# The last row of w_down in two halves with 64-column matmuls, and the last 4 MB of w_o as one load

One core of one Trainium2 chip. The metric is the device time of one execution in microseconds, lower is better. In the views PE is the matrix engine (PEld its weight loads), DVE the vector engine, ACT the scalar engine, and SP the one whose queue issues the loads. A matmul is two records: LDWEIGHTS for one operand, the weights, and MATMUL for the other, the moving operand.

## The reference, cut to what matters

One decode step of a block: adaLN modulation, attention over a cache of 65,536 positions, output projection with w_o, layer norm, then a gated feed-forward layer. The change touches the last line, and the projection with `wo` before it.

```python
x = x + ga * _A_ref(h, A_k_cache, A_v_cache, A_wq, A_wo)      # wo: 4096 x 1024
h = _layernorm(x, axis=-1) * (1 + cb) + sb
x = x + gb * _B_ref(h, B_w_gate, B_w_up, B_w_down)            # w_down: 3584 x 1024
```

There is one token, so every product is a vector by a matrix, and the kernel is a stream of 185.6 MB of weights and cache out of HBM.

## The kernel before

The weights go to ten slots of 2 MB. A load is planned in order, and SP issues it once the slot's last readers are done. `w_down` is used in 28 "rows" of 128 x 1,024: rows 0 to 19 as the moving operand against a 32-column weight ("row form"), the last eight as the weights themselves ("column form"):

```python
def col_matvec(bank, jobs, rhs, nblk, first):          # column form; nblk = KD = 8, D = 1024
    for (jb, view, k0, nk) in jobs:
        PE.wait(jb.tok)
        for kk in range(nk):
            for j in range(nblk):
                ins = pe.matmul(
                    bank[:, j:j + 1], view[:, kk, j:D:nblk], rhs[:, k0 + kk:k0 + kk + 1], ...)
        tok = PE.done(ins)
        release(jb, tok)
    ...
```

`view[:, kk, j:D:nblk]` is the weight: 128 columns, each 8 elements from the next, so that output `8 p + j` lands in partition `p`, column `j`. The moving operand is one column. The end of the kernel:

```python
v = row_matvec(place_d, early, o_pad, (v_uc,), ...)     # rows 0 to 19
# ... DVE transposes the sums of the row form (1.3 us)
late = j_d[len(early):]                                 # loads of rows 20-21, 22-23, 24-25, 26, 27
col_matvec(acc_dn, late[:1], o_pad[:, :, 0], KD, True)
PE.wait(v_rows, v_sel)
for a in range(NQ):                                     # adds the transposed sums to acc_dn
    pe.matmul(acc_dn[QD * a:QD * (a + 1), :], sel32[:, :], turned[:, a, :, 0], ...)
v = col_matvec(acc_dn, late[1:], o_pad[:, :, 0], KD, False)
DVE.wait(v)
# ... two DVE products and sums of 128 x 8, then the output DMA
```

Of the kernel before, what the change touches and what calls it, by code (L numbers as in the profile page):

```python
# [9 lines left out]
P = 128  # L10
# [8 lines left out]
UE = 4  # L19
# [3 lines left out]
ROW = 512  # L23
# [57 lines left out]
def bass_adaLN_cond__gqa_block_cached__geglu_ffn__decode_kernel(  # L81
# [14 lines left out]
    D = A_x.shape[-1]  # L96
    KD = D // P
# [7 lines left out]
    FD = F // P  # L105
# [13 lines left out]
    PE = Eng(nc, nc.tensor, "c_pe")  # L119
# [3 lines left out]
    sp, pe, dve, act, pool = nc.sync, nc.tensor, nc.vector, nc.scalar, nc.gpsimd  # L123
# [24 lines left out]
    o_pad = p_row[:, :, :].rearrange("p a b -> p (a b)").rearrange("p (k c) -> p k c", c=QD)  # L148
# [41 lines left out]
    acc_dn = b7[:, 64:64 + KD]  # L190
# [9 lines left out]
    def plan_load(src, view_fn, slot, site=None, nslot=1, beside=None, off=0, sem=None):  # L200

        if site is not None:
            site.n += 16
            tok = (site.sem, site.n)
        else:
            sem = slot if sem is None else sem
            nfill[sem] += 1
            tok = (fill[sem], 16 * nfill[sem])
        job = Job(view_fn(slot_all[:, slot * SLOT + off:(slot + nslot) * SLOT]), tok, slot)
        job.src = src  # L210
        job.freed = None
        job.prev = []
        if beside is not None:
            job.prev = beside.prev
        for t in range(slot, slot + (nslot if beside is None else 0)):
            if last_job[t] is not None and last_job[t] not in job.prev:
                job.prev.append(last_job[t])
            last_job[t] = job
        loads.append(job)
        return job  # L220
# [3 lines left out]
    def issue_ready():  # L224

        while issued[0] < len(loads):
            j = loads[issued[0]]
            if any(q.freed is None for q in j.prev):
                return
            SP.wait(*(q.freed for q in j.prev))  # L230
            sp.dma_start(j.view, j.src).then_inc(j.tok[0], 16)
            issued[0] += 1
# [3 lines left out]
    def release(job, tok):  # L236
        job.freed = tok
        if not in_loop[0]:
            issue_ready()

    def flat(nk, n):
        return lambda t: t[:, 0:nk * n].rearrange("p (k n) -> p k n", k=nk)

    def emit_all():
# [5 lines left out]
        wo_v = A_wo.rearrange("(p k) n -> p k n", p=P)  # L250
        wg_v = B_w_gate.rearrange("(p k) n -> p k n", p=P)
        wu_v = B_w_up.rearrange("(p k) n -> p k n", p=P)
        wd_v = B_w_down.rearrange("(b p e) n -> p b e n", p=P, e=UE)
# [3 lines left out]
        def kv_src(h, i, n=1):  # L257
            g, cc = divmod(i, NCH)
            return h[g][:, cc * CH:(cc + n) * CH, :]
# [2 lines left out]
        j_mod = [(plan_load(wmod_v[:, k:k + 2, :], flat(2, M6), next(head), nslot=2), k, 2) for k in range(0, KD, 2)]  # L262
        j_q = [(plan_load(wq_v[:, k:k + 4, :], flat(4, HQ * DH), next(head), nslot=2), k, 4) for k in range(0, KD, 4)]
        tail = iter([2, 4, 6, 8])
        tail_d = iter([0, 1, 2, 3, 4, 5])

        def plan_o(k, slot):
            return (plan_load(wo_v[:, k:k + 8, :], flat(8, D), slot), k, 8)

        def vslot(j):  # L270
            return SITES + j % SITES
# [10 lines left out]
        j_o = []  # L282
        for i in range(0, NC + KU, KU):
# [6 lines left out]
            if i >= KU:  # L290
                j = i - KU
                j_v[j] = plan_load(kv_src(vh, j, VU), flat(VU * CH, DH), vslot(j), vfill[j % SITES // VU], VU)
        j_o += [plan_o(16, 0), plan_o(24, 1)]
        j_g = [(plan_load(wg_v[:, k:k + 4, :], flat(4, F), next(tail), nslot=2), k, 4) for k in range(0, KD, 4)]
        j_u = [(plan_load(wu_v[:, k:k + 4, :], flat(4, F), next(tail), nslot=2), k, 4) for k in range(0, KD, 4)]
        j_d = []
        NBF = FD // UE
        b = 0
        NROW = NBF - 2
        while b + 2 < NROW:  # L300
            jb = plan_load(
                wd_v[:, b:b + 2, :, :],
                lambda t: t[:, 0:2 * UE * D].rearrange("p (b e n) -> p b e n", b=2, e=UE),
                next(tail_d),
            )
            j_d.append((jb, jb.view.rearrange("p b e n -> p (b e) n"), b * UE, 2 * UE))
            b += 2
        while b < NBF:
            for e, ne in ((0, UE),) if b < NROW else ((0, 2), (2, 2)) if b == NROW else ((0, 2), (2, 1), (3, 1)):
                if b == NROW:  # L310
                    jb = plan_load(
                        wd_v[:, b, e:e + ne, :], flat(ne, D), jb.slot, beside=jb, off=(UE + e) * D, sem=9 - e)
                else:
                    jb = plan_load(wd_v[:, b, e:e + ne, :], flat(ne, D), next(tail_d))
                j_d.append((jb, jb.view, b * UE + e, ne))
            b += 1
# [28 lines left out]
        for a in [a for r in ev for a in r] + ex + m1 + oc + pc + kfill + vfill:  # L345
# [10 lines left out]
        v = DVE.done(dve.tensor_reduce(  # L356
            dm4.unsqueeze(3), identf[:, :].rearrange("p (c b h) -> p c b h", c=NQ, h=REP), AX.X, ALU.add))
# [8 lines left out]
        for j in range(KD):  # L366
            ins = pe.matmul(b6[:, 2 * j:2 * j + 2], cx_row[:, j:D:KD], ident[0:2, 0:2], start=True, stop=True)
        v = PE.done(ins)
# [5 lines left out]
        v = DVE.done(dve.tensor_scalar(sg_col[:, :], th_col[:, :], 0.5, 0.5, ALU.mult, ALU.add))  # L374
# [3 lines left out]
        def col_matvec(bank, jobs, rhs, nblk, first):  # L378

            tok = None  # L380
            for (jb, view, k0, nk) in jobs:
                PE.wait(jb.tok)
                ins = None
# [3 lines that stand above are left out]
                            bank[:, j:j + 1], view[:, kk, j:D:nblk], rhs[:, k0 + kk:k0 + kk + 1],  # L387
                            start=first, stop=True, skip_group_check=True,
                        )
                        first = False  # L390
                tok = PE.done(ins)
                release(jb, tok)
            return tok

        def whole(jobs):
            return [(jb, jb.view, k0, nk) for jb, k0, nk in jobs]
# [69 lines left out]
        def turn(dst, w, src, cols, n, ready):  # L466

            PE.wait(*ready)
            for i, a in enumerate(cols):
                ins = pe.transpose(dst[:, i * w:i * w + n], src[:, a], identf[0:src.shape[0], 0:n])  # L470
            return PE.done(ins)
# [37 lines left out]
        def place_2(b0, n):  # L509
            def place(k):  # L510
                for c in range(n):
                    yield quad(b0 + c // NQ, c % NQ), c * ROW
            return place

        v = row_matvec(place_2(0, 2 * NQ), whole(j_q), h_pad, (v_h,), (0, KD - 1), rest_of_mod)
# [4 lines left out]
        v = turn(tr_ps, P, row_q, plain, P, (v_ra, v_rb))  # L520
        DVE.wait(v)
        v = DVE.done(dve.tensor_copy(
            q_col[:, :].rearrange("p (r g t) -> p r t g", r=2, g=NQ),
            quads(tr_ps, KD).rearrange("p (r t) g -> p r t g", r=2)))
# [243 lines left out]
        for g in range(Hkv):  # L768
            ins = pe.matmul(
                b6[0:HQ, 0:P + ZW], selw[:, HQ - REP * (g + 1):HQ - REP * (g + 1) + QD], o_red[:, g, :],  # L770
                start=g == 0, stop=g == Hkv - 1)
        v = PE.done(ins)
        DVE.wait(v)
        v = DVE.done(dve.reciprocal(rz[:, :], b6[0:HQ, P + ZW - 1:P + ZW]))
        DVE.wait(v)
        v = DVE.done(dve.tensor_scalar(oT[:, :], b6[0:HQ, 0:P], rz[:, 0:1], None, ALU.mult))
        PE.wait(v, v_const)
        w = P // QW
        for q in range(QW):
            ins = pe.matmul(  # L780
                b6[:, 352:352 + w], spread[:, QW - 1 - q:QW - 1 - q + P], oT[:, q * w:(q + 1) * w],
                start=q == 0, stop=q == QW - 1)
        v = PE.done(ins)
# [16 lines left out]
        v = row_matvec(place_o, whole(j_o), o_pad, (v_opk,) + last_ev, (NQ - 1, HQ - NQ))  # L800
        t_att = sb("t_att", [P, KD])
        v_rows = both(row_a, 0, P)
        v = turn(tr_ps, P, row_a, mixed, P, v_rows)
# [3 lines left out]
        v = DVE.done(dve.tensor_tensor(t_att[:, :], t_att[:, :], mod_sb[:, 2, :], ALU.mult))  # L807
        DVE.wait(v)
        v_x1 = DVE.done(dve.tensor_tensor(x1_col[:, :], t_att[:, :], x_col, ALU.add))
        hn2, v = ln_norm(x1_col[:, :], v_x1, 34)  # L810
        v_h2 = modulate(h_pad, hn2, v, 3, 4)
        NBF = F // ROW
# [15 lines left out]
        v = row_matvec(place_2(2, NBF), whole(j_g), h_pad, (v_h2,), (0, KD - 1))  # L828
# [3 lines left out]
        for dst, src in zip(parts(g1), parts_ps()):  # L832
            v = DVE.done(dve.tensor_copy(dst, src))
        v_g1 = v
        DVE.wait(v)
        v = DVE.done(dve.tensor_tensor(g2, g1, g1, ALU.mult))
        DVE.wait(v)
        v = DVE.done(dve.tensor_scalar(g3, g2, GELU_C, 1.0, ALU.mult, ALU.add))
        DVE.wait(v)
        v = DVE.done(dve.tensor_tensor(g4, g3, g1, ALU.mult))  # L840
        AC.wait(v)
        v = AC.done(act.activation(gth, g4, ACT.Tanh, scale=SQRT_2_OVER_PI))
        DVE.wait(v)
        v = DVE.done(dve.scalar_tensor_tensor(g2, gth, 1.0, g1, ALU.add, ALU.mult))
        v_g2 = v
        v = row_matvec(place_2(0, NBF), whole(j_u), h_pad, (v_h2,), (0, KD - 1))
# [10 lines left out]
        v = row_matvec(place_d, early, o_pad, (v_uc,), (NQ - 1, NROW * UE - NQ))  # L857
# [5 lines left out]
        late = j_d[len(early):]  # L863
# [3 lines left out]
        for a in range(NQ):  # L867
            pe.matmul(
                acc_dn[QD * a:QD * (a + 1), :], sel32[:, :], turned[:, a, :, 0],
                start=False, stop=True, skip_group_check=True)  # L870
        v = col_matvec(acc_dn, late[1:], o_pad[:, :, 0], KD, False)
        DVE.wait(v)
        v = DVE.done(dve.tensor_tensor(t_dn, acc_dn, mod_sb[:, 5, :], ALU.mult))
        DVE.wait(v)
        v = DVE.done(dve.tensor_tensor(y_col, t_dn, x1_col[:, :], ALU.add))
# [3 lines left out]
        assert issued[0] == len(loads)  # L879

    emit_all()
    return nc

# [27 lines left out]
```

## Time and profile before

| | before |
|---|---|
| time, median of 3 runs | 437.55 us (437.49 to 437.65) |
| span of the profiled run | 436.2 us |
| HBM read | 185.60 MB, 426 GB/s over the span |
| DMA queue of the loads, share of the 16 engines | 99.0% |
| PE, DVE, ACT busy | 69%, 47%, 26% |
| last landing of w_down, to DVE's next step | 433.40 us, to 434.32 us |

The 99.0% say that the transfers set the length up to their last byte. What comes after the last landing is the loose part at this end, and it is about 2.8 us of 436.2. The views that show it stand in the prediction. A *landing* is the time at which the sixteenth and last of the DMA engines has counted up a load's semaphore. The *beat* is the time from the start of one matmul to the start of the next.

### The profile page before, as it was taken

The page shows a single profiled execution, that of the slowest core. Times are in us where ns is not written, and L with a number is a line of the kernel's source. Part 1 is how long each engine was busy: PE and PEld are TensorE (multiplying, and loading weights), DVE is VectorE, ACT ScalarE, POOL GpSimd, SP SyncE. Part 2 cuts the span into 40 slices and gives each one's busy share as a digit, 9 for nine tenths or more (in the row PEclk, how much of TensorE's full clock was granted, in tenths as well). Part 3 has the DMA queues.
Part 4 walks back from the last instruction along what each step waited for, and adds up shares of the span by engine and source line. Part 5 has one row for each costly group of instructions (what it writes and reads, how often), then busy time and mean ns, then how long its engine had stood idle before and what let it go on. Part 6 is the DMA issues. An engine that isn't in the chain of part 4 may idle for free.

```text
span 436.2 us, 8423 instructions
## 1 busy us (share of the span) xinstructions
PE 302.8 (69%) x3858; PEld 200.5 (46%) x3858; DVE 206.7 (47%) x303; ACT 111.2 (26%) x164; POOL 16.8 (4%) x23
## 2 busy tenths in 40 slices
PE   0435559959696878949787794969689596565366
PEld 0112236736464656636465563646456373232024
DVE  6601015637373755736474763738377465321001
ACT  1000001533332423333341353333235334000000
POOL 9500000000000000000000000000000000000000
PEclk9995569999796988988896897969689889578856
DMA  8999999999999999999999999999999999999996
GB/s 355 433 421 434 433 431 431 431 432 433 433 433 439 430 433 433 436 433 433 439 433 433 433 430 436 433 436 436 433 433 433 433 418 436 437 433 429 420 425 265
DMA packets 8192, 185.77 MB, mean 426 GB/s; under 512 B 1010, under 2 KB 1010, under 8 KB 1652
## 3 DMA queue, kind: packets, MB, share of 16 engines
q1 hardware_dynamic: 8176, 185.60, 99.0%
q8 instruction: 8, 0.13, 0.1%
q14 instruction: 4, 0.03, 0.0%
q10 hardware_dynamic: 4, 0.00, 0.0%
HBM read 185.60 MB, written 0.00 MB: 426 GB/s over the span
## 4 chain that ended last, share of the span: by engine, by line
DMA 56%; PE 31%; DVE 11%; issue 1%; ACT 1%; POOL 0%; POOLq 0%
DMA slots<-in_A_k_cache_dram 45%; PE kt_ps L575 16%; DMA slots<-in_B_w_down_dram 7%; PE b L645 4%; DMA slots<-in_A_v_cache_dram 4%; PE sc_ps L597 4%; PE kt_ps L409 3%; DVE selt L359 3%; DVE kt_sb L683 2%; DVE s_pad L717 1%; DVE o_red L706 1%; PE sc_ps L626 1%; PE b L613 1%; PE b L386 1%; DVE o_acc L694 1%
## 5 line engine op out<-in xcount | busy, mean ns | idle before, releaser
L575 PE MATMUL kt_ps<-ident,slots 128*128 128x128 bf16 x2048 | 156.7, 238 | 48.8 <-DMA slots<-in_A_k_cache_dram 48.0
L683 DVE COPY kt_sb<-kt_ps 128x2048 bf16<-128x2048 bf16 x96 | 117.6, 1225 | 111.5 <-PE kt_ps L575 109.9
L575 PEld LDWEIGHTS kt_ps<-ident,slots 128*128 128x128 bf16 x2048 | 136.1, 108 | 74.3 <-issue 41.9
L683 ACT ACTIVATE kt_sb<-kt_ps 128x2048 bf16<-128x2048 bf16 x32 | 60.1, 1877 | 27.7 <-PE kt_ps L575 27.7
L732 ACT ACTIVATE p_sb<-sc_ps 128x512 bf16<-128x512 bf16 x32 | 19.1, 597 | 182.4 <-PE sc_ps L626 182.4
L597 PE MATMUL sc_ps<-kt_sb,q_buf 128*32 128x512 bf16 x528 | 50.8, 420 | 0.0
L645 PE MATMUL b<-slots,p_sb 128*32 128x512 bf16 x560 | 40.1, 411 | 5.3 <-DMA slots<-in_A_v_cache_dram 4.6
L409 PE MATMUL kt_ps<-slots,h_pad 128*32 128x512 bf16 x176 | 19.1, 571 | 22.0 <-DMA slots<-in_B_w_up_dram 9.7
L694 DVE SCALAR_TENSOR_TENSOR o_acc<-o_acc,s_pad,b 128x512 f32<-128x512 f32 x28 | 20.9, 747 | 12.2 <-PE b L645 11.9
L613 PE MATMUL b<-m_sp,selt 128*128 128x16 f32 x66 | 13.0, 272 | 18.2 <-DVE m_sp L722 16.5
L645 PEld LDWEIGHTS b<-slots,p_sb 128*32 128x32 bf16 x560 | 15.5, 104 | 20.1 <-issue 5.1
L717 DVE TENSOR_REDUCE s_pad<-sc_ps 128x1 f32<-128x512 f32 x32 | 21.8, 682 | 0.0
L738 ACT ACTIVATE p_row<-sc_ps,s_pad 128x512 bf16<-128x512 f32 x32 | 21.7, 677 | 0.0
L409 PEld LDWEIGHTS kt_ps<-slots,h_pad 128*32 128x32 bf16 x176 | 6.3, 130 | 32.7 <-issue 11.9
L613 PEld LDWEIGHTS b<-m_sp,selt 128*128 128x128 f32 x66 | 9.8, 188 | 23.7 <-DVE m_sp L722 21.4
L597 PEld LDWEIGHTS sc_ps<-kt_sb,q_buf 128*32 128x32 bf16 x528 | 10.9, 95 | 12.3 <-issue 4.5
L409 PE MATMUL kt_ps<-slots,s_pad 128*32 128x512 bf16 x96 | 10.9, 516 | 7.5 <-DMA slots<-in_w_mod_dram 7.5
L452 POOL TENSOR_TENSOR rs<-va,halfneg 128x1 f32<-128x1 f32 x2 | 1.1, 555 | 375.7 <-DVE va L449 375.7
L793 DVE COPY kt_sb<-kt_ps 128x512 f32<-128x512 f32 x3 | 2.1, 692 | 27.7 <-PE kt_ps L409 27.7
L626 PEld LDWEIGHTS sc_ps<-ident,p_row 128*128 128x128 bf16 x136 | 7.8, 98 | 15.1 <-issue 14.4
L626 PE MATMUL sc_ps<-ident,p_row 128*128 128x128 bf16 x136 | 13.7, 224 | 0.2 <-ACT p_row L738 0.2
L727 DVE TENSOR_REDUCE s_pad<-b 128x1 f32<-128x16 f32 x32 | 5.6, 175 | 14.6 <-PE b L613 14.6
(98 smaller groups left out, 148.1 us busy)
## 6 DMA issues: line engine op xcount, KB each, us to landing
slots<-in_A_k_cache_dram SPq DMA_DIRECT2D x16, 4096.0 KB, 23.5
slots<-in_A_v_cache_dram SPq DMA_DIRECT2D x16, 4096.0 KB, 23.6
slots<-in_w_mod_dram SPq DMA_DIRECT2D x4, 3072.0 KB, 20.4
slots<-in_A_wq_dram SPq DMA_DIRECT2D x2, 4096.0 KB, 35.8
slots<-in_A_wo_dram SPq DMA_DIRECT2D x4, 2048.0 KB, 25.3
slots<-in_B_w_gate_dram SPq DMA_DIRECT2D x2, 3584.0 KB, 30.2
slots<-in_B_w_up_dram SPq DMA_DIRECT2D x2, 3584.0 KB, 29.5
slots<-in_B_w_down_dram SPq DMA_DIRECT2D x2, 2048.0 KB, 35.1
```

The source lines that it names most:

```text
L359: dve.tensor_scalar(selt[:, :].rearrange("p (r h) -> p r h", h=REP), selw[:, HQ - REP:HQ].unsqueeze(1).to_broadcast([P, NR, REP]), -scale, ...
L409: ins = pe.matmul(out, pad[:, k, :], view[:, kk, c0:c0 + ROW], start=k <= last_k[0], stop=k >= last_k[1], skip_group_check=True,)
L575: ins = pe.transpose(kt_ps[:, half * 2048 + t * P:half * 2048 + (t + 1) * P], j_k[i - i % KU].view[:, i % KU * CH + b * TB + t, :], ident[ ...
L597: ins = pe.matmul(sc(j)[QD * g:QD * (g + 1), :], q_buf[:, j % SITES, QD * b:QD * (b + 1)], kt_sb[:, j % 2, n:n + w, :].rearrange("p n d -> ...
L613: ins = pe.matmul(b6[:, 0:NR], selt[:, :], m_sp[:, j % 2, :], start=True, stop=True)
L626: ins = pe.transpose(sc_bf[:, o:o + P], p_row[:, j % 2, c * P:(c + 1) * P], ident[:, :])
L645: ins = pe.matmul(b7[QD * c:QD * (c + 1), :].rearrange("p (b d) -> p b d", b=NB), p_sb[:, s, c * P + QD * g:c * P + QD * (g + 1)], v[:, NQ ...
L683: ev[i % SITES][b].done(act.activation(dst, src, ACT.Copy) if E_ is AC else dve.tensor_copy(dst, src))
L694: v = oc[j % SITES].done(dve.scalar_tensor_tensor(o_acc[:, :], o_acc[:, :], al[:, j:j + 1], b7[:, :], ALU.mult, ALU.add))
L717: v = DVE.done(dve.tensor_reduce(m_new, sc(j), AX.X, ALU.max))
L732: pc[jt % SITES].done(act.activation(p_sb[:, jt % SITES, :], sc_bf[:, o:o + ROW], ACT.Copy))
L738: v_x[j] = ex[s].done(act.activation(p_row[:, j % 2, :], sc(j), ACT.Exp, bias=mneg[:, j:j + 1], scale=scale, accum_out=zr[:, j:j + 1],))
```

## The change

The intent: PE should have less left to do when the last bytes arrive. The last 256 KB come as two halves of 512 columns, and each half is used as it lands; only the second half's 8 smaller matmuls are left after the last landing. A weight of 512 columns gives 64 columns at a step of 8, so these 8 matmuls write half of the partitions. One load is added, and the two last loads of w_o become one.

```diff
...
-        def plan_o(k, slot):
-            return (plan_load(wo_v[:, k:k + 8, :], flat(8, D), slot), k, 8)
+        def plan_o(k, slot, n=8):
+            return (plan_load(wo_v[:, k:k + n, :], flat(n, D), slot, nslot=n // 8), k, n)
...
-        j_o += [plan_o(16, 0), plan_o(24, 1)]
+        j_o.append(plan_o(16, 0, 16))
...
+                elif b + 1 == NBF and e + 1 == UE:
+                    halves = [plan_load(
+                        wd_v[:, b, e:e + 1, h * ROW:(h + 1) * ROW], flat(1, ROW), next(tail_d)) for h in range(2)]
+                    break
...
-        v = col_matvec(acc_dn, late[1:], o_pad[:, :, 0], KD, False)
+        col_matvec(acc_dn, late[1:], o_pad[:, :, 0], KD, False)
+        for h, jb in enumerate(halves):
+            PE.wait(jb.tok)
+            for j in range(KD):
+                ins = pe.matmul(
+                    acc_dn[h * P // 2:(h + 1) * P // 2, j:j + 1], jb.view[:, 0, j:ROW:KD], o_pad[:, FD - 1:FD, 0],
+                    start=False, stop=True, skip_group_check=True)
+            v = PE.done(ins)
+            release(jb, v)
```

More of the change, by code (lines that the diff above doesn't have):

```diff
@@ L264, in emit_all @@
         tail = iter([2, 4, 6, 8])
-        tail_d = iter([0, 1, 2, 3, 4, 5])
-        def plan_o(k, slot):
-            return (plan_load(wo_v[:, k:k + 8, :], flat(8, D), slot), k, 8)
+        tail_d = iter([0, 1, 2, 3, 4, 5, 6])
+        def plan_o(k, slot, n=8):
+            return (plan_load(wo_v[:, k:k + n, :], flat(n, D), slot, nslot=n // 8), k, n)
         def vslot(j):
```

## The prediction

The sum of the prediction came to -0.08 + 0.51 + 0.07 = +0.50 us. The 62 ns for a matmul of 64 columns, from which the +0.51 comes, stand as the author's estimate, from the 60 ns measured for 128 columns and the 51 to 64 ns that the loads of L470 suggest. The 7 ns between a matmul's start and the next weight load make the 107 ns under the rivals into 114. "Four chunks" stands for the recorded access [32, 1, 4]; that 64 columns would not be read so was an assumption. The "change of tiling mode" is the change from matmuls of one weight width to another, with its 133 ns in the trace.

> **What bounds the kernel now.** I read the page first, then the last 50 us in order of time, then the last 8 us, because both edits touch only what comes after the attention loop.
>
> From the page of the kernel before, three rows over 40 slices of 10.9 us each (PE clock in tenths, mean busy share of the DMA engines in tenths, GB/s):
>
> ```profile
> PEclk9995569999796988988896897969689889578856
> DMA  8999999999999999999999999999999999999996
> GB/s 355 433 421 434 433 431 431 431 432 433 433 433 439 430 433 433 436 433 433 439 433 433 433 430 436 433 436 436 433 433 433 433 418 436 437 433 429 420 425 265
> ```
>
> The DMA engines are full from the second slice to the last but one. 185.60 MB at some 430 GB/s is 432 us of the 436.2 us span, so nothing in the middle can be gained except by moving fewer bytes or paying less per packet. Only the two ends are loose. The change touches the far end, so I go there: the waits for w_down and for w_o, then the timeline.
>
> Waits of the kernel before from 429 us on (engine, line, what it waited for, us in total, times, longest):
>
> ```profile
> DVE kt_sb L873 <- PE b L386: 3.5, 1, 3.5
> PE kt_ps L409 <- DMA slots<-in_B_w_down_dram: 1.4, 1, 1.4
> PEld b L386 <- DMA slots<-in_B_w_down_dram: 1.1, 1, 1.1
> PE b L386 <- DMA slots<-in_B_w_down_dram: 0.2, 1, 0.2
> ```
>
> Timeline of the kernel before from 428 us on (start, length, engine, line, operation, tile, shape, count):
>
> ```profile
> 428.42 1.06 PE L409 MATMUL kt_ps<-slots,p_row 128*32 128x512 bf16 x8 [1.38 <-DMA slots<-in_B_w_down_dram]
> 429.55 1.31 DVE L860 STREAM_TRANSPOSE kt_sb<-kt_ps 128x512 f32<-128x512 f32 x2 [6.81 <-PE kt_ps L409]
> ...
> 430.92 0.29 PE L868 MATMUL b<-kt_sb,sel 128*32 128x8 f32 x8
> ...
> 431.14 3.14 PE L386 MATMUL b<-p_row,slots 128*128 128x1 bf16 x48
> 434.32 0.17 DVE L873 TENSOR_TENSOR kt_sb<-b,mod_sb 128x8 f32<-128x8 f32 x1 [3.46 <-PE b L386]
> 434.52 0.17 DVE L875 TENSOR_TENSOR kt_sb<-kt_sb,x_col 128x8 bf16<-128x8 f32 x1
> 434.72 0.35 SPq L877 DMA_DIRECT2D out_dram<-kt_sb  x1
> ```
>
> The reader is to see that the 48 last matmuls run as one block of 3.14 us with no idle time in front of any of them that the view reports. They belong to four loads: rows 22 and 23 (16 matmuls), rows 24 and 25 (16), row 26 (8), row 27 (8). The semaphore records of the trace, read one by one, give the full landings of those loads: 430.89, 432.13, 432.76 and 433.40 us. The matmul records give the first matmul of each: 431.14, 432.18, 433.18 and 433.66 us. So PE really waits for the second of them (the matmul comes 0.05 us after the landing, and the gap in front of it is 95 ns where 60 is usual). For the third and fourth, the ones that matter here, the data lies ready: row 26 for 0.42 us, row 27 for 0.26 us. After the last landing at 433.40 us PE works until 434.28 us, and DVE, the output DMA and its receipt follow. **The end is set by PE's backlog of column matmuls, not by the last transfer.** DMA bounds it one step earlier, through the loads that landed at 428.38 (rows 16 to 19) and 432.13 us.
>
> Each of the 64 column matmuls costs 60 ns start to start (median of 62 gaps in the records), and the load of its weights 170 ns, of which all but 60 overlaps. The granted clock is 0.50 from 427.7 us on.
>
> [...] the L386 weights are read so: their recorded access is [32, 1, 4]. [...] The nearest rows of the trace are strided fp32 loads of L470 at full clock: 93 to 129 ns apart for 128 columns, some 0.8 to 1.0 ns a column, so 51 to 64 ns for 64 columns. [...] no 64-column weight load is in the trace.
> [...] The trace has such a change, from the 32-column matmuls of L868 to the 128-column ones of L386: 133 ns between the last start of one and the first of the other, 73 more than the usual 60, though the data had landed 0.25 us before.
> [...] The packets here: 84 ns for 2,048 B, 159 for 4,096, 309 for 8,192, 611 for 16,384 and 1,213 for 32,768. That is 9 ns plus 36.7 ns per 1,024 B.
>
> **The change part by part.**
>
> *The last row in two halves, transfers.* One load of 128 packets of 2,048 B becomes two of 128 packets of 1,024 B. Each of the 16 DMA engines moves 16 packets of 9 + 37 = 46 ns (estimate by the line above) in place of 8 of 84 ns, and one semaphore packet of 9 ns more: 745 against 672, so about +0.08 us. The first half should land about 0.35 us before the second, so at some 433.1 us.
>
> *The w_o load.* Two loads of 128 packets of 16,384 B become one of 128 packets of 32,768 B. Per engine 8 x 1,213 = 9,704 ns replace 16 x 611 = 9,776 ns, and one semaphore packet goes: -0.08 us of transfer time. The queue is never empty from there on, so everything that lands later lands 0.08 us sooner; the chain hangs on the landing at 428.38, and so it moves by -0.08. The two w_o loads landed at 377.36 and 382.21 us, and the matmuls that read them began only at 383.53, released by DVE (attention's end). So waiting for 4 MB at once costs nothing there. The release of the first of the two slots comes up to 0.86 us later (w_down's first issues were at 387.94 and 388.80); what they fetch landed at 421 us, behind two w_up loads still queued. No effect.
>
> *The slot of the second half.* It is slot 6, held by the first half of w_up until its matmuls end, near 411 us. The issue of row 27 was at 413.57 us in the trace[...]; the new one follows at some 416 to 418 us, 15 us before its data is due. No effect.
>
> *The last matmuls.* 8 matmuls with 128-column weights become 16 with 64 columns, each with one moving column. PE comes to them with the data lying there, so all the added work is exposed. If a 64-column pair costs what a 128-column one does, 60 ns [...], 8 more cost 8 x 60 = +0.48 us; at 68 ns all 16 cost 16 x 68 - 8 x 60 = +0.61. I take 62: +0.51. The change of tiling mode in front of them: +0.07. The second wait is met already and costs nothing: between the third and fourth group before, where a wait also stood and was met, the gap was 60 ns.
>
> Sum: -0.08 + 0.51 + 0.07 = +0.50 us. The last landing (+0.08 - 0.08 = 433.4 us) stays behind PE's start of the second half, 433.58 + 0.07 + 8 x 0.062 = 434.15 us, so it binds nowhere.
>
> **The rivals.**
>
> *The intended gain: only half a row is left to do after the last landing.* It would hold if PE waited for the last transfer. For it: DMA bounds the whole kernel, and each 64-column matmul might cost half of a 128-column one (30 ns). Against it: PE is 0.26 us late already, so shortening the work behind the last landing shortens nothing; at 30 ns for 64 columns PE's total is merely unchanged. Then the time would be 437.55 - 0.08 + 0.07, so 437.5 us.
>
> *Strided 64-column weights load far slower.* The columns of w_down are 8 elements apart. The four-chunk load of 32 such columns takes 53 ns (from weight load to matmul start, in the records), 1.7 ns for a column of a chunk. Without the four chunks, 64 columns at 1.7 ns are 107 ns. For it: that figure. Against it: strided fp32 loads run at 0.8 to 1.0 ns a column. It would make 16 x 114 - 480 = +1.3 us, so 438.9 us.
>
> *The transfers become the bound again.* If small packets cost more than the line says, the last landing slips. It must slip by 0.75 us to matter, twice what the whole half takes. Against it: 2,048 B packets fit the same line as 32,768 B ones. At most some tenths, 437.8 to 438.3 us.
>
> *Something upstream shifts*, for example the w_o merge letting the 0.08 us through or not: within 437.5 to 438.2.
>
> **Range and chances.** The runs before lie within 0.16 us of each other, so the range is set by the cost of a 64-column pair: 30 ns gives 437.5, 62 gives 438.05, 114 gives 438.9. I put most weight on 55 to 75 ns, so 438.0, and 437.4 to 438.8 for 8 in 10. Two per cent would be 8.75 us, more than all the time behind the landing at 428.38 us, so a verdict other than "same" needs something unforeseen: 0.005 faster, 0.99 same, 0.005 slower.
>
> **What would show it right or wrong.** Right: in the changed kernel's timeline, 40 matmuls of 128 columns and then 16 of 64 columns without DMA idle in front of them, spaced about 60 ns apart; the span from the w_down landing that releases the 512-column matmuls to DVE's product with the gate (L873 before) longer by about 0.6 us; that landing itself some 0.1 us earlier. Wrong: a wait for DMA in front of the second half (then transfers bind), 16 matmuls in 0.5 us (then the columns are what costs), or in 1.8 us (then the stride is). A longer w_o wait before the matmuls that read it would also refute the neutrality of the merge.

## The result

The changed kernel took 438.53 us (median of 6 runs, 438.49 to 438.64); the kernel before, beside it, 437.53 us (437.47 to 437.65). The ratio is 1.0023, with a 95% interval from 1.001 to 1.0036: 1.0 us slower, which counts as the same at the 2% line. Ratios here and below are those from the runs of both kernels in the same rounds; they are not quite the ratio of the medians quoted.

The change shifts the line numbers: L386, L409, L868 and L873 of before are L390, L413, L872 and L885 of after; L879 is new and holds the narrow matmuls. The timeline of the changed kernel at its end (start, length, engine, line, operation, tile, shape, count):

```profile
428.42 1.05 PE L413 MATMUL kt_ps<-slots,p_row 128*32 128x512 bf16 x8 [0.54 <-DMA slots<-in_B_w_down_dram]
...
431.13 2.66 PE L390 MATMUL b<-p_row,slots 128*128 128x1 bf16 x40
433.72 1.54 PEld L879 LDWEIGHTS b<-p_row,slots 128*64 128x64 bf16 x16
433.73 1.62 PE L879 MATMUL b<-p_row,slots 128*64 128x1 bf16 x16
435.38 0.17 DVE L885 TENSOR_TENSOR kt_sb<-b,mod_sb 128x8 f32<-128x8 f32 x1 [4.54 <-PE b L879]
```

The release at 428.42 us and the 40 wide matmuls from 431.13 us stand where they stood before. The whole difference is the last block: 16 narrow matmuls in 1.62 us, and DVE at 435.38 instead of 434.32 us. The waits of the changed kernel from 429 us on (four of six lines; the other two are on L864 and L872):

```profile
DVE kt_sb L885 <- PE b L879: 4.5, 1, 4.5
PEld b L390 <- DMA slots<-in_B_w_down_dram: 1.1, 1, 1.1
PE kt_ps L413 <- DMA slots<-in_B_w_down_dram: 0.5, 1, 0.5
PE b L390 <- DMA slots<-in_B_w_down_dram: 0.2, 1, 0.2
```

No line of the view has L879 waiting for a DMA: the two halves landed at 433.07 and 433.40 us, and PE came to the first at 433.72. Then the narrow instructions themselves (durations in ns as minimum, median, maximum), first of the kernel before, where L386 is the wide form:

```profile
L386 PEld LDWEIGHTS b<-p_row,slots x64: 141/171/177, 429.7 to 434.0; 128*128 128x128 bf16 x64
```

and of the changed kernel, where L879 is the narrow one:

```profile
L879 PEld LDWEIGHTS b<-p_row,slots x16: 192/217/217, 433.7 to 435.0; 128*64 128x64 bf16 x16
L879 PE MATMUL b<-p_row,slots x16: 257/258/279, 433.7 to 435.1; 128*64 128x1 bf16 x16
```

A weight load of half as many columns takes 217 ns where the whole one took 171. The records give the beat: 60 ns for the wide matmuls, 120 ns for the narrow ones of one half. They give the sum as well. From the last wide start to the first narrow one 128 ns, 68 over the usual 60. From the first narrow start to the last 1.36 us, where the 8 wide ones took 0.42: +0.94. The last matmul lasts 258 ns instead of 198: +0.06. Together +1.07 us, against 1.06 between the two starts of DVE's step.

### The profile page after: what moved, and what is told of

Read it like the earlier page. It is cut to its first block, busy times and chain, and to the rows that moved or that the text cites. A ratio compares the mean times of both kernels' runs of the same rounds, so it can differ in the third digit from the quotient of the medians.

```text
span 437.2 us, 8439 instructions
## 1 busy us (share of the span) xinstructions
PE 307.5 (70%) x3866; PEld 201.9 (46%) x3866; DVE 206.7 (47%) x303; ACT 111.2 (25%) x164; POOL 16.8 (4%) x23
## 4 chain that ended last, share of the span: by engine, by line
DMA 55%; PE 32%; DVE 11%; issue 1%; ACT 1%; POOL 0%; POOLq 0%
DMA slots<-in_A_k_cache_dram 44%; PE kt_ps L579 16%; DMA slots<-in_B_w_down_dram 7%; PE b L649 5%; PE sc_ps L601 4%; DMA slots<-in_A_v_cache_dram 4%; PE kt_ps L413 4%; DVE selt L363 3%; DVE kt_sb L687 2%; DVE s_pad L721 1%; DVE o_red L710 1%; PE sc_ps L630 1%; PE b L617 1%; DVE o_acc L698 1%; PE b L390 1%
## 5 line engine op out<-in xcount | busy, mean ns | idle before, releaser
L601 PE MATMUL sc_ps<-kt_sb,q_buf 128*32 128x512 bf16 x528 | 51.7, 426 | 0.0
L649 PE MATMUL b<-slots,p_sb 128*32 128x512 bf16 x560 | 41.9, 425 | 5.1 <-DMA slots<-in_A_v_cache_dram 4.4
L413 PE MATMUL kt_ps<-slots,h_pad 128*32 128x512 bf16 x176 | 19.7, 586 | 22.6 <-DMA slots<-in_A_wq_dram 9.8
L413 PEld LDWEIGHTS kt_ps<-slots,h_pad 128*32 128x32 bf16 x176 | 6.4, 130 | 33.4 <-issue 11.9
L413 PE MATMUL kt_ps<-slots,s_pad 128*32 128x512 bf16 x96 | 11.0, 521 | 7.1 <-DMA slots<-in_w_mod_dram 7.1
```

What stands on the lines that cost most here:

```text
L413: ins = pe.matmul(out, pad[:, k, :], view[:, kk, c0:c0 + ROW], start=k <= last_k[0], stop=k >= last_k[1], skip_group_check=True,)
L601: ins = pe.matmul(sc(j)[QD * g:QD * (g + 1), :], q_buf[:, j % SITES, QD * b:QD * (b + 1)], kt_sb[:, j % 2, n:n + w, :].rearrange("p n d -> ...
L649: ins = pe.matmul(b7[QD * c:QD * (c + 1), :].rearrange("p (b d) -> p b d", b=NB), p_sb[:, s, c * P + QD * g:c * P + QD * (g + 1)], v[:, NQ ...
```

## The experiments

Theory A, after the result: all of it lies in the narrow matmuls, and nothing in the transfers. Its rival B: the transfers moved, and part of the 1.0 us is theirs. Within A there are two more: S, that the narrow weights load slowly because their columns lie apart; and W, that within half of the array a weight load has to wait for the matmul before it, wherever the columns lie.

| run | time, us | before in its rounds, us | ratio (95% interval) |
|---|---|---|---|
| e1_wo_only | 437.54 | 437.53 | 1.0 (0.9986 to 1.0013) |
| e2_halves_128 | 437.55 | 437.53 | 1.0001 (0.9987 to 1.0014) |
| e3_mm64_only | 438.72 | 437.53 | 1.0023 (1.0009 to 1.0037) |
| e4_interleaved | 438.07 | 437.53 | 1.0011 (0.9997 to 1.0025) |
| e5_contig64 | 437.74 | 437.51 | 1.0005 (0.999 to 1.0021) |
| e6_cols120 | 438.74 | 437.51 | 1.0029 (1.0014 to 1.0044) |
| e7_contig128 | 437.31 | 437.51 | 0.9997 (0.9982 to 1.0012) |
| e8_warm | 437.62 | 437.51 | 1.0001 (0.9987 to 1.0015) |
| e9_contig_before | 437.02 | 437.52 | 0.9989 (0.9975 to 1.0002) |
| e10_contig_after | 437.36 | 437.52 | 0.9996 (0.9983 to 1.001) |
| e11_single_rows | 437.66 | 437.52 | 1.0 (0.9986 to 1.0014) |
| e12_single_rows_plain | 437.44 | 437.6 | 0.9997 (0.9984 to 1.0011) |

The intervals are as wide as the effects (0.001 is 0.44 us), so where a few tenths matter I go by the timeline and the records and use the times as a check. e5, e7, e9 and e10 give a wrong result on purpose, and so does e6, though its error was too small to be noticed.

### The parts one by one: e1, e2, e3

e1, the w_o load alone:

```diff
-        j_o += [plan_o(16, 0), plan_o(24, 1)]
+        j_o.append(plan_o(16, 0, 16))
```

> The kernel before with the last 4 MB of w_o as one load and nothing else. Theory A (all of the +1.0 us lies in the 16 narrow matmuls): 0.0 us against before, within 0.1; the prediction on record said -0.08 us. Rival B (the transfers moved): w_o's merge delays w_down's first loads and costs 0.2 us or more.

437.54 against 437.53 us. The last landing was at 433.41 us, against 433.40, and the one that releases the last 512-column matmuls at 428.42, against 428.38. Neither the cost of rival B nor the 0.08 us gained in the prediction is seen. But 0.08 us is too little to rule out here: in the other profiles of kernels with the loads of before, that landing lies anywhere from 428.33 (e6) to 428.69 us (e3).

e2, the two half loads alone, used by 128-column matmuls once both have landed:

```diff
+    jb = plan_load(wd_v[:, b, e:e + 1, 0:ROW], half(0), s)
...
+    jb2 = plan_load(wd_v[:, b, e:e + 1, ROW:D], half(1), s, own, beside=jb)
...
-    v = col_matvec(acc_dn, late[1:], o_pad[:, :, 0], KD, False)
+    col_matvec(acc_dn, late[1:-1], o_pad[:, :, 0], KD, False)
+    PE.wait(late[-1][0].tok, jb2.tok)
+    v = col_matvec(acc_dn, late[-1:], o_pad[:, :, 0], KD, False)
```

> The kernel before with the last row of w_down loaded in two halves of 512 columns, but still used by 8 matmuls of 128 columns after both have landed. Theory A: 0.0 us against before, within 0.1, the 8 matmuls 60 ns apart, no wait in front of them. Rival B: +0.3 us or more, with a DMA wait in front of the last 8 matmuls. The prediction on record had +0.08 us for the last landing, hidden behind PE.

437.55 against 437.53 us, and the 48 wide matmuls (L396 in this run) ran through without a DMA wait in 3.18 us:

```profile
431.14 3.18 PE L396 MATMUL b<-p_row,slots 128*128 128x1 bf16 x48
434.35 0.17 DVE L885 TENSOR_TENSOR kt_sb<-b,mod_sb 128x8 f32<-128x8 f32 x1 [3.50 <-PE b L396]
```

Halving the load costs nothing that can be seen in the time.

e3, the 16 narrow matmuls alone, out of one whole load:

```diff
-    v = col_matvec(acc_dn, late[1:], o_pad[:, :, 0], KD, False)
+    col_matvec(acc_dn, late[1:-1], o_pad[:, :, 0], KD, False)
+    jb = late[-1][0]
+    PE.wait(jb.tok)
+    for h in range(2):
+        for j in range(KD):
+            ins = pe.matmul(
+                acc_dn[h * P // 2:(h + 1) * P // 2, j:j + 1],
+                jb.view[:, 0, h * ROW + j:(h + 1) * ROW:KD], o_pad[:, FD - 1:FD, 0], ...)
```

> The kernel before with its one load of the last row, but used by 16 matmuls of 64 columns, all of the first half and then all of the second. Theory A: +1.0 us against before (0.9 to 1.1), the pairs 120 ns apart within a half, some of the two halves side by side. Rival B: +0.5 us or less.

438.72 against 437.53 us, ratio 1.0023 as for the whole change. The timeline of e3 has the same block as the changed kernel:

```profile
434.06 1.62 PE L876 MATMUL b<-p_row,slots 128*64 128x1 bf16 x16
```

Its median is 0.2 us above the changed kernel's and outside the 0.9 to 1.1 us expected. The profiled run (438.88 us) had its landings some 0.3 us later, the last one at 433.71 us; the block of narrow matmuls is the same.

So theory A holds and B falls: the cost is the 16 narrow matmuls, whatever the loads.

### What a narrow matmul waits for: e4 to e7

e4 takes the two halves in turn, after both have landed:

```diff
-        for h, jb in enumerate(halves):
-            PE.wait(jb.tok)
-            for j in range(KD):
+        PE.wait(*(jb.tok for jb in halves))
+        for j in range(KD):
+            for h, jb in enumerate(halves):
```

> The changed kernel, but the two halves taken in turn: column 0 of the first half, column 0 of the second, column 1 of the first and so on, after both have landed. If the 120 ns are a wait within one half of the array (a weight load waits for the matmul before it in the same half) and the halves run side by side, the 16 take 8 x 120 = 0.96 us: +0.55 us against before, so 0.45 us faster than the changed kernel. If PE is simply occupied 120 ns by each, 16 x 120 = 1.92 us: +1.5 us against before. If each takes 60 ns when no pair follows in its own half, 0.96 us too; the order of starts tells the two apart (26 ns offsets in a 120 ns beat, or an even 60 ns).

438.07 us, +0.54. The timeline of e4:

```profile
433.75 1.12 PE L879 MATMUL b<-p_row,slots 128*64 128x1 bf16 x16
```

In the records the starts come in pairs, 6 ns apart, every 120 ns. So the 120 ns are a wait inside one half of the array, and the two halves run side by side. This also explains why the changed kernel did not need 15 x 120 ns = 1.80 us from first start to last but 1.36: in its records the second half's matmuls begin at 434.23 us, while the last of the first half starts at 434.58. PE did not keep the order of the program here: the matmul that waits for the second load's semaphore started 0.36 us before the last one of the first half, which comes before it in the program.

e5 takes the narrow weights from neighbouring columns:

```diff
-                    ... jb.view[:, 0, j:ROW:KD] ...
+                    ... jb.view[:, 0, j * 64:(j + 1) * 64] ...
```

> The changed kernel with the 64 weight columns of each narrow matmul taken side by side instead of 8 elements apart (the result is wrong on purpose). Theory S (the stride is what costs once the weights are no longer read in four chunks, 1.7 ns a column): the beat within a half falls from 120 to 55 to 70 ns, the 16 take about 1.0 us, and the time is 438.0 us. Rival W (in a half of the array a weight load waits for the matmul before it, whatever the stride): the beat stays at 105 to 120 ns and the time at 438.5 us.

The beat in a half fell from 120 to 53 or 54 ns. The narrow instructions of e5:

```profile
L879 PEld LDWEIGHTS b<-p_row,slots x16: 128/157/158, 433.7 to 434.3; 128*64 128x64 bf16 x16
```

The weight load fell from 217 to 157 ns and the block to 0.83 us; the time was 437.74 us, 0.26 less than expected: the beat came out below the 55 to 70 ns of the expectation, and the halves again ran side by side for part of the block, which I had not counted. W said 105 to 120 ns, so W falls.

e6 is the wide form with 120 columns in place of 128, and e7 the wide form with neighbouring columns, both for the last row only:

```diff
-    v = col_matvec(acc_dn, late[1:], o_pad[:, :, 0], KD, False)
+    col_matvec(acc_dn, late[1:-1], o_pad[:, :, 0], KD, False)
+    # e6: acc_dn[0:120, j:j + 1], jb.view[:, 0, j:120 * KD:KD]
+    # e7: acc_dn[:, j:j + 1],     jb.view[:, 0, j * P:(j + 1) * P]
```

> The kernel before with the last 8 matmuls cut to 120 of 128 columns, still 8 elements apart, over the whole width of the array (the result is wrong on purpose). Such a weight should no longer be read in four chunks. Theory S: some 200 ns a matmul (120 x 1.7), 8 of them +1.1 us against before. If it is the half-width mode alone that costs: 60 ns and 0.0 us. If the loss of the chunks costs but not the stride: 100 to 110 ns and +0.4 us.

> The kernel before with the 128 weight columns of the last 8 matmuls side by side (the result is wrong on purpose). Theory S: the chunked load is slowed by the stride as well, so 25 to 35 ns a matmul instead of 60, -0.2 to -0.28 us, unless the last landing at 433.4 us stops it first. If the stride costs nothing in the chunked load: 60 ns and 0.0 us.

e6 has a beat of 220 ns and a time of +1.23 us; e7 has 27 ns and -0.20 us. First the weight loads of e6, then of e7:

```profile
L875 PEld LDWEIGHTS b<-p_row,slots x8: 308/317/317, 433.5 to 435.1; 128*120 128x120 bf16 x8
```

```profile
L875 PEld LDWEIGHTS b<-p_row,slots x8: 103/104/138, 433.7 to 433.9; 128*128 128x128 bf16 x8
```

In e6 no half is used alone, and the first matmul comes 60 ns after the wide one before it. Still, eight columns fewer make the load 317 ns instead of 171. The recorded access shows the difference: [32, 1, 4], four chunks of 32 columns, for 128 columns, but [120, 1, 1] for 120 and [64, 1, 1] for 64. Put together:

| weight | read as | beat, columns side by side | beat, columns 8 apart | ns per column of a chunk |
|---|---|---|---|---|
| 128 columns | 4 chunks of 32 | 27 ns (e7) | 60 ns (before) | 0.84, 1.88 |
| 64 columns | 1 chunk of 64 | 53.5 ns (e5) | 120 ns (changed) | 0.84, 1.88 |
| 120 columns | 1 chunk of 120 | not run | 220 ns (e6) | 1.83 |

One reading fits all five beats: the beat of a one-column matmul is the time to read the longest chunk of its weight, 0.84 ns a column side by side, some 1.85 at a step of 8. With 64 columns a chunk is twice as long as with 128, so there are twice as many matmuls, each of twice the beat, and only their running side by side gives some of it back. So S holds, but it is half of the cause: the step of 8 makes wide and narrow loads alike 2.2 times slower, and that a narrow one takes twice a wide one, at either step, comes with the loss of the four chunks. No run tried a step other than 1 and 8. All five beats were taken at a granted clock of 0.50 (the eight 512-column matmuls before them took 1.05 or 1.06 us in each of the five profiles; at 1.00, in e8, 0.62).

### Is it the clock? e8

In the kernel before the granted clock is 0.50 from 427.7 us on. e8 keeps PE at work in its waits:

```diff
+                for _ in range(fill_in[n] if fill_in else 0):      # 3 and 3, ahead of two waits; 1 more later
+                    pe.matmul(b6[:, :], ident[:, :], p_sb[:, 0, :], start=True, stop=True)
                 PE.wait(jb.tok)
```

> The kernel before with 7 idle 512-column matmuls on known data put into PE's waits for w_down from 424 to 429.7 us[...] (the result is unchanged). If the clock is 1.0 after 428 us and the column matmuls depend on it: the beat falls from 60 to 30 to 45 ns, PE catches up with the last landing, and the time falls by 0.4 to 0.8 us. If the strided weight load does not depend on the granted clock: the beat stays at 55 to 60 ns, only the 512-column matmuls shorten, -0.1 to -0.4 us. If the clock stays at 0.5: 0.0 us, or up to +0.2 us where the added matmuls are in the way.

The time did not move (437.62 against 437.51 us), but the run answers the question: its granted clock was 1.00 from 424 us on. That the idle matmuls raised it is not shown: from 420 to 424 us, with the first of them only at the end, it was 0.99 already, against 0.50 in the kernel before. Stretches of the kernel before with its L386 instructions (length, PE busy and count, PE weight load busy and count, granted clock, DMA share, GB/s):

```profile
431.00:433.70 2.70, 2.56 (x41) 2.56 (x42) 0.50 0.49 188
```

and of e8:

```profile
431.00:433.70 2.70, 2.51 (x39) 2.44 (x40) 1.00 0.49 190
```

The clock is double, and nearly as many matmuls fit into the stretch (39 in place of 41, since e8 waited 0.2 us longer for a landing within it): the beat in the records is 60 ns in both. So here the strided load of 128 columns did not follow the granted clock (60 ns at 0.50 and at 1.00); for columns side by side and for 64 columns this was not run. What did follow it are the 512-column matmuls, eight in 0.62 us where they took 1.06; but what they gained ended at the next landing, at 432.29 us, behind which the same 32 column matmuls of 60 ns remain.

### The intended gain, where PE does wait: e9 and e10

Both kernels with all column matmuls on neighbouring columns, so that PE keeps up with the transfers:

```diff
-                    bank[:, j:j + 1], view[:, kk, j:D:nblk], ...
+                    bank[:, j:j + 1], view[:, kk, j * P:(j + 1) * P], ...
```

and in e10, besides, the edit of e5.

> The kernel before with all 64 column matmuls reading their weight columns side by side (the result is wrong on purpose), so that PE is no longer behind the transfers. Theory S: 27 ns a matmul, PE waits for each of the last loads, and the time is the last landing (433.4 us) plus 8 x 27 ns and the rest: -0.4 us against before, so 437.1 us, with a DMA wait in front of the last 8 matmuls. If something else than the strided weight loads held the end, less than -0.1 us.

> The changed kernel with all its column matmuls reading their columns side by side (the result is wrong on purpose): the halves, tried where PE does wait for the last transfer. The intended gain (less is left to do after the last landing) would make it as fast as e9_contig_before or up to 0.1 us faster. Theory S: what is left after the last landing is 8 x 54 ns in place of 8 x 27 ns, so 0.1 to 0.25 us slower than e9_contig_before: 437.2 to 437.4 us.

437.02 us for e9, -0.5 us against before; 437.36 us for e10. Every run of e9 lies between 436.98 and 437.23, every run of e10 between 437.18 and 437.46; their intervals overlap. The timeline of e9:

```profile
433.57 0.37 PE L386 MATMUL b<-p_row,slots 128*128 128x1 bf16 x8 [0.27 <-DMA slots<-in_B_w_down_dram]
433.98 0.17 DVE L873 TENSOR_TENSOR kt_sb<-b,mod_sb 128x8 f32<-128x8 f32 x1 [3.00 <-PE b L386]
```

and of e10:

```profile
433.10 0.90 PE L879 MATMUL b<-p_row,slots 128*64 128x1 bf16 x16
434.03 0.17 DVE L885 TENSOR_TENSOR kt_sb<-b,mod_sb 128x8 f32<-128x8 f32 x1 [3.22 <-PE b L879]
```

In e9 PE waits for the last landing (433.52 us in that run), and DVE starts 0.46 us after it. In e10 the first half is worked on as it lands, which is what the change wanted; the last landing was at 433.36 us, and DVE starts 0.67 us after it. So halving loses even where its premise is met, by 0.2 us in the profile: 8 matmuls at 54 ns remain in place of 8 at 27. And e9 shows what the step of 8 costs the kernel before: half a microsecond (0.46 us from the last landing to DVE's step, against 0.92). A kernel with side-by-side columns and a right result, which would need the output laid out otherwise, was not tried.

### Something that beats both? e11 and e12

The last four rows as four single loads, so that PE need not wait for rows 24 and 25 together; e11 with the idle matmuls of e8, e12 without:

```diff
-    ... ((0, 2), (2, 1), (3, 1)):
+    ... ((0, 1), (1, 1), (2, 1), (3, 1)):
```

> A candidate to beat both, with a right result: the kernel before with the last four rows of w_down as four single-row loads, so that PE need not wait for two rows at once, and the 7 idle matmuls of e8_warm. If PE's 48 column matmuls of 60 ns after the landing of rows 22 and 23 are the whole of the end, the waits between them vanish and it gains 0.1 to 0.2 us against before: 437.35 us. If the idle matmuls or the smaller loads cost as much, 0.0 us.

e11 missed: 437.66 against 437.52 us. Its timeline:

```profile
427.84 1.46 PE L405 MATMUL b<-p_sb,ident 128*128 128x512 bf16 x3
...
431.50 3.05 PE L386 MATMUL b<-p_row,slots 128*128 128x1 bf16 x48
```

This time the clock was 0.5 when the three idle matmuls ran; they took 1.46 us (0.82 in e8) and held up the 512-column matmuls, whose data had landed at 428.38 us, until 429.23.

> The kernel before with its last four rows of w_down as four single-row loads and no idle matmuls (the result is right). In e11_single_rows the idle matmuls ran at half clock and held up the 512-column matmuls by 0.85 us; without them the column matmuls should start at 431.1 us as before and run through without a wait: 48 x 60 ns, so -0.05 to -0.15 us against before, 437.4 to 437.5 us. That is less than five rounds resolve by time; the timeline has to show it (48 matmuls in 3.02 to 3.07 us in place of 3.14, no DMA wait in front of them).

e12 took 437.44 against 437.60 us. Its timeline:

```profile
431.27 3.05 PE L386 MATMUL b<-p_row,slots 128*128 128x1 bf16 x48
```

The wait for two rows is gone and the block is 3.05 instead of 3.14 us, which is all that cutting the last four rows into single loads can give. Whether the time follows, five rounds can't tell (0.9984 to 1.0011). So there is no version with a right result here that is shown to beat the kernel before.

## Why the prediction was right or wrong

*What bounds the end.* Right. PE's backlog of column matmuls sets it: no DMA wait stands in front of L879, e2 costs nothing, and e9, where PE is no longer late, gains 0.5 us. Of its 0.46 us in the profile 0.22 are the backlog (the last row's first matmul starts 0.05 us after the landing, not 0.27), the rest the eight shorter matmuls behind it.

*The loads.* The neutral parts were right: the late slot (the second half was issued at 416.29 us, within the 416 to 418 foreseen), and w_o, which landed at 382.17 us while the matmuls that read it began at 383.56, after DVE. The two terms of 0.08 us were not borne out. The -0.08 for w_o stands in the sum and is not seen: the landing that releases the last 512-column matmuls came at 428.37 us, against 428.38. The +0.08 for the halves (0.07 by its own figures, 745 less 672) was rightly kept out of the sum, as PE was late anyway, but it too was oversized. Averaged over the 16 engines, the last row took 0.64 us as 8 packets of 2,048 B (0.63 to 0.65 in the nine profiles with a whole last row) and 0.67 us as 16 packets of 1,024 B (0.67 to 0.69 in five), where adding up the packets' durations gives 0.67 and 0.74 us. The prediction took the 9 ns that a packet lasts beyond its bytes as time of the queue; most of it overlaps with the neighbouring packets: 0.640 and 0.665 us, with nine packets more for each engine, make some 3 ns a packet (estimate from these two). Its line was a little off as well: 37.5 ns per 1,024 B fits its five durations, not 36.7.

*The change of tiling mode.* +0.07 us predicted, +0.068 measured. The 128 ns between the last wide start and the first narrow one stand in the changed kernel, e3, e4 and e5 alike, whatever the step; where no half is used alone (e6, e7) it is 60 and 61 ns.

*The last matmuls.* Here is the step that failed: "If a 64-column pair costs what a 128-column one does, 60 ns", of which the prediction took 62 ns and +0.51 us. Measured were 120 ns and +1.00 us (0.94 of beats and 0.06 of the last matmul's length). I took the cost of a column from strided fp32 loads in other places (L470, 0.8 to 1.0 ns), though the rows to be changed had their own figure in the same trace: 53 ns for a chunk of 32 columns. (Most records have 58 ns there, and 2 ns to the next load where the prediction read 7; the sum is 60 either way, but 58 would have given 118 ns for 64 columns.) The figure of 53 ns was used in the second rival, which made it 114 ns and 438.9 us. Its mechanism is the right one by e5, e6 and e7. Its sum overshot by 0.4 us because it let the 16 matmuls run one after the other, and nearly half a microsecond of them (1.80 less 1.36) ran side by side in the two halves of the array (e4 shows this by itself).

*Sum.* Predicted -0.08 + 0.51 + 0.07 = +0.50 us (438.05, rounded to 438.0); in the profile 0 + 1.00 + 0.07, and +1.00 in the time. That the range of 437.4 to 438.8 held was luck. The rival that came true stands outside it with its 438.9, and the 438.53 measured lies inside only because the two halves ran side by side, which no part of the prediction foresaw: 120 ns one after the other would have come to some 439.0 us (estimate, 438.53 and the 0.44 us saved). "Same" was right with a wide margin, 1 us of 8.75.

*The intended gain* was refuted twice: PE was late anyway, as predicted, and e10 shows that it would lose where PE is not late, which was not foreseen.

## What to carry to other kernels

Before splitting a last transfer, look whether anything waits for it: compare the landing with the start of its first reader. Here halving the columns of a 128-column bf16 weight gave up the read in four chunks (recorded access [64, 1, 1] in place of [32, 1, 4]), and a one-column matmul got twice as long, not half (120 ns in place of 60). Such a weight is better left whole; a cut by rows did no harm here (e12), but no gain in time was shown either. Where the weights are the large operand and the moving one is a single column, the step between weight columns is worth a look: here a step of 8 took 60 ns for what took 27 ns side by side.
